# Luna attention and SiLU MLP on one core: other early order, w_out scaled without GpSimd, ones of v written once

## The chip, the core and the metric

The kernel runs on one core of a Trainium2 chip. Its engines are TensorE (PE, with its weight loads as PEld), VectorE (DVE), ScalarE (ACT), GpSimd (POOL) and SyncE (SP, which issues the DMAs). The metric is the device time of one execution in microseconds (us), the median of three runs; lower is better.

## The reference, cut to what matters

```
p_packed = softmax(p @ k.T / 8) @ v          # 8 batches x 8 heads, 576 tokens, head size 64, 32 packed rows
attn     = softmax(q @ p_packed.T / 8) @ p_packed
x        = attn, heads side by side           # 4608 tokens x 512
h        = x @ w_in                           # w_in 512 x 2048
g        = h * sigmoid(beta * h)              # beta: one number per hidden column
out      = g @ w_out                          # w_out 2048 x 512, float32
```

All inputs come as float32; the kernel multiplies in bfloat16 and adds up in float32.

## The kernel before, in words

The eight batches pass one after the other through the same steps, and neighbours overlap. In the names of the program, with b the batch:

- `ld` loads k, v and q of a batch, `cast` turns them to bfloat16 (k_bf, v_bf, q_bf). Batches 0 and 1 are cast by any of three engines and turned by PE (`tr`, `trr`, copied out by `T`, `rk`, `rq`); from batch 2 on POOL casts and a DMA transposes (`tr` on SP, tiles kT and qT).
- `s1`, `e1`, `pun`, `pp` form the packed rows; `s2`, `e2`, `z2`, `l2`, `n2`, `A2` the second softmax (tile A2T).
- `w`, `W`: the second attention product and the input product are fused: PE multiplies the packed rows with w_in (tile w_ps), DVE scales by beta into W_bf.
- `h`, `g`: for each of 16 blocks of 128 hidden columns PE computes A2T x W_bf (two matmuls of 512 columns, tile h_ps), ACT applies SiLU into g_main. `hr`, `gr` do the same for the 64 tokens left over.
- Output: batch 0 multiplies g by w_out plainly (`o`, with `take` and `add` on DVE). Batches 1 to 7 and the left-over tokens use a Strassen scheme with seven products (`p`, `P`): DVE first forms sums of blocks of w_out (`T4`, tile w_sum) and of g (`S`, tile g_sum), and reads the products out (`R`).

Since `W` holds beta, `w_out` is divided by it: each of 16 blocks of w_out is multiplied by `rbeta` while it is cast (line 1469, `cast_out`), on DVE, ACT or POOL. w_in and w_out come in four loads each (`ld_in`, `ld_out`) through three staging buffers, so a load waits until the casts of the load three places earlier are done.

What each engine does, and in which order, is written out by hand in the table `SEQUENCE`; a planner walks the five lists, and its estimated durations decide only how instructions of different engines are interleaved, where the activation tables are switched, and where PE gets fill products. `HOME` says from which ring of PSUM banks a step takes its bank: "h" (2 banks), "o" (2 banks) or "att" (4 banks). A fill product is a 128x128 matmul of ones whose result nobody reads; the planner puts some wherever it expects PE to wait in the first 60 us, if a bank of ring "o" is free:

```
if len(opened) >= n and (opened[-n][0] is None or opened[-n][0] > free["PE"]):
    return
...
        self.filler()
```

Each engine works its list strictly in order, SP too, and the wait of a list's head holds all that stands behind it. Lines 421 and 426 are helpers: every matmul has line 421 and every transpose on PE line 426.

Of the kernel before, what the change touches and what calls it, by code (L numbers as in the profile page):

```python
# [8 lines left out]
B, H, S, D = 8, 8, 576, 64  # L9
# [39 lines left out]
PE_BATCHES = 2  # L49
def TILED(key):  # L50
# [13 lines left out]
    ("brow", 0): "o",  # L64
    ("brow", 2): "o",
    ("brow", 3): "att",
    ("tr", 0, "q", 1): "h",
    ("s1r", 0): "o",
    ("s1", 0, 0): "h",
    ("s1", 0, 1): "h",  # L70
    ("z1", 0): "o",
    ("s2", 0, 1): "h",
    ("z2", 0, 0): "o",
    ("z2", 0, 1): "o",
    ("z2", 0, 2): "o",
    ("w", 0, 0): "o",
    ("tr", 1, "k", 0): "o",
    ("tr", 1, "k", 1): "h",
    ("tr", 1, "q", 0): "o",
    ("s1", 1, 1): "h",  # L80
    ("s2", 1, 0): "h",
    ("z2", 1, 0): "h",
    ("z2", 1, 1): "h",
# [305 lines left out]
class Kernel:  # L389
# [70 lines left out]
    def plan_loads(self, b):  # L460
        nc = self.nc
        rank = 100 * b
        early = b < PE_BATCHES
        for xi, x in enumerate("kqv" if b == 0 else "kvq"):
# [39 lines left out]
            old = self.readers(b - 1, x)  # L504
# [1047 lines left out]
```

## Time and profile before

| | |
|---|---|
| median of 3 runs | 240.79 us (240.64 to 241.34) |
| the profiled execution | 241.07 us |
| its span, first to last instruction | 239.3 us |
| around the span | 1.77 us |
| mean granted TensorE clock | 0.986 |
| last PE matmul ends | 235.6 us |

Durations in the text come from the profiled execution. Busy time is a sum over the span; what ends a wait is inferred from semaphores. A granted clock of 1.00 is the 2.4 GHz level of TensorE, 0.50 the 1.2 GHz level. "PE busy" is not PE at its peak: matmuls are pipelined, and one that is late counts as busy.

### The profile page before, as it was taken

The page shows a single profiled execution, that of the slowest core. Times are in us where ns is not written, and L with a number is a line of the kernel's source. Part 1 is how long each engine was busy: PE and PEld are TensorE (multiplying, and loading weights), DVE is VectorE, ACT ScalarE, POOL GpSimd, SP SyncE. Part 2 cuts the span into 40 slices and gives each one's busy share as a digit, 9 for nine tenths or more (in the row PEclk, how much of TensorE's full clock was granted, in tenths as well). Part 3 has the DMA queues.
Part 4 walks back from the last instruction along what each step waited for, and adds up shares of the span by engine and source line. Part 5 has one row for each costly group of instructions (what it writes and reads, how often), then busy time and mean ns, then how long its engine had stood idle before and what let it go on. Part 6 is the DMA issues. An engine that isn't in the chain of part 4 may idle for free.

```text
span 239.3 us, 6112 instructions
## 1 busy us (share of the span) xinstructions
PE 224.5 (94%) x2550; PEld 152.9 (64%) x2576; DVE 160.9 (67%) x254; ACT 171.3 (72%) x312; POOL 82.5 (34%) x90
## 2 busy tenths in 40 slices
PE   7887899986999999999999999999999999999993
PEld 6554353333477765775588567876786578677883
DVE  4569647884897945986798855852788279515751
ACT  3619679874899977977679678896788679665300
POOL 3223448398873160624151730540354000000000
PEclk9999589999999999999999999999999999999999
DMA  6999999999999999999999899969794040022044
GB/s 216 396 387 399 401 350 348 290 325 224 263 263 191 274 275 245 218 320 242 230 279 331 225 236 303 225 128 221 160 313 147 3 175 3 1 86 92 0 122 144
DMA packets 67107, 54.14 MB, mean 226 GB/s; under 512 B 38948, under 2 KB 58532, under 8 KB 66568
## 3 DMA queue, kind: packets, MB, share of 16 engines
q1 hardware_dynamic: 67072, 53.75, 81.5%
q8 instruction: 20, 0.33, 0.6%
q14 instruction: 7, 0.06, 0.1%
q10 hardware_dynamic: 8, 0.01, 0.0%
HBM read 37.23 MB, written 9.44 MB: 195 GB/s over the span
## 4 chain that ended last, share of the span: by engine, by line
PE 72%; DMA 11%; POOL 5%; ACT 4%; DVE 3%; issue 2%; SPq 1%; POOLq 0%; DVEq 0%
PE o_ps L421 42%; PE h_ps L421 19%; DMA k<-in_k_dram 6%; DMA w_in<-in_moe_w_in_dram 5%; POOL w_out_bf L1469 3%; PE w_ps L421 3%; PE hr_ps L421 3%; PE s_ps L421 2%; PE pp_ps L421 1%; PE z_ps L421 1%; ACT g_main L992 1%; POOL k_bf L515 1%; DVE g_main L1223 1%; DVE W_bf L957 1%; ACT L438 1%
## 5 line engine op out<-in xcount | busy, mean ns | idle before, releaser
L992 ACT ACTIVATE g_main<-h_ps 128x512 bf16<-128x512 f32 x128 | 72.2, 596 | 34.9 <-PE h_ps L421 28.1
L421 PEld LDWEIGHTS <-g_main 128*128 128x128 bf16 x624 | 58.8, 98 | 25.8 <-issue 5.3
L421 PE MATMUL h_ps<-A2T,W_bf 128*128 128x512 bf16 x233 | 68.5, 390 | 1.8 <-DVE A2T L890 1.0
L421 PE MATMUL o_ps<-w_out_bf,g_main 128*128 128x256 bf16 (+1 forms) x397 | 61.2, 289 | 2.3 <-POOL w_out_bf L1469 1.9
L421 PEld LDWEIGHTS <-W_bf 128*128 128x128 bf16 x512 | 33.2, 99 | 20.6 <-issue 6.6
L950 DVE TENSOR_TENSOR W_bf<-w_ps,beta_bc 128x512 bf16<-128x512 f32 x48 | 30.6, 684 | 15.8 <-PE w_ps L421 15.8
L421 PE MATMUL o_ps<-w_sum,g_sum 128*128 128x256 bf16 x256 | 33.1, 273 | 0.6 <-DVE o_sb L1253 0.4
L421 PE MATMUL o_ps<-w_sum,g_main 128*128 128x256 bf16 x224 | 31.3, 273 | 0.3
L1253 DVE TENSOR_TENSOR o_sb<-o_ps,o_sb 128x512 f32<-128x512 f32 (+1 forms) x27 | 17.0, 630 | 18.9 <-PE o_ps L421 15.6
L438 ACT ACT_TABLE_LOAD x22 | 28.2, 1283 | 1.1 <-PEq L1536 0.7
L421 PEld LDWEIGHTS <-g_sum 128*128 128x128 bf16 x256 | 24.3, 98 | 6.3 <-issue 1.0
L515 POOL CAST q_bf<-q 128x1024 bf16<-128x1024 f32 x12 | 13.6, 1151 | 31.2 <-DMA q<-in_q_dram 31.2
L515 POOL CAST v_bf<-v 128x1024 bf16<-128x1024 f32 x12 | 15.6, 1326 | 22.4 <-DMA v<-in_v_dram 22.4
L1255 ACT COPY o_sb<-o_ps 128x512 f32<-128x512 f32 (+1 forms) x16 | 8.1, 506 | 14.1 <-PE o_ps L421 14.1
L515 POOL CAST k_bf<-k 128x1024 bf16<-128x1024 f32 x12 | 13.3, 1124 | 12.8 <-DMA k<-in_k_dram 12.8
L1255 DVE COPY o_sb<-o_ps 128x512 f32<-128x512 f32 (+1 forms) x20 | 13.2, 661 | 4.1 <-PE o_ps L421 4.0
L957 DVE SCALAR_TENSOR_TENSOR W_bf<-w_ps,rz,beta_bc 128x512 bf16<-128x512 f32 x15 | 10.4, 745 | 4.2 <-PE w_ps L421 4.2
L890 DVE TENSOR_TENSOR A2T<-E2T,rz 128x512 bf16<-128x512 bf16 x16 | 11.6, 733 | 2.1 <-ACT rz L885 1.8
L1469 POOL TENSOR_SCALAR w_out_bf<-w_out,rbeta 128x512 bf16<-128x512 f32 x6 | 10.6, 1768 | 4.8 <-DMA w_out<-in_moe_w_out_dram 4.7
L1223 DVE TENSOR_TENSOR g_sum<-g_main 128x2048 bf16<-128x2048 bf16 x7 | 9.0, 1283 | 3.9 <-ACT g_main L992 3.9
L421 PE MATMUL w_ps<-w_in_bf,pp 64*32 64x512 bf16 x252 | 11.1, 389 | 0.0
L873 ACT ACTIVATE rz<-z_ps 128x512 f32<-128x512 f32 x16 | 9.6, 604 | 1.9 <-PE z_ps L421 1.9
(131 smaller groups left out, 281.3 us busy)
## 6 DMA issues: line engine op xcount, KB each, us to landing
k<-in_k_dram SPq DMA_DIRECT2D x6, 1024.0 KB, 8.7
v<-in_v_dram SPq DMA_DIRECT2D x6, 1024.0 KB, 8.3
q<-in_q_dram SPq DMA_DIRECT2D x6, 1024.0 KB, 9.2
out_dram<-o_sb SPq DMA_DIRECT2D x10, 512.0 KB, 3.7
w_in<-in_moe_w_in_dram SPq DMA_DIRECT2D x4, 1024.0 KB, 11.5
w_out<-in_moe_w_out_dram SPq DMA_DIRECT2D x4, 1024.0 KB, 10.7
out_dram<-o_sb SPq DMA_DIRECT2D x12, 256.0 KB, 3.8
k<-in_k_dram SPq DMA_DIRECT2D x4, 576.0 KB, 6.4
```

The costliest lines, as they stand in the source:

```text
L421: return self.nc.tensor.matmul(out, lhsT, rhs, start=start, stop=stop, tile_position=pos, skip_group_check=True)
L438: self.nc.scalar.preload_act_table_set(SETS[mode])
L515: self.copy[engine](o[:, 0 : 32 * e].rearrange("p (t h e) -> p h t e", t=4, h=8)[:, h, :, 0:D], t[:, 0:2048].rearrange("p (h t d) -> p h t ...
L873: nc.scalar.activation(st[b, "rz2"][:, i], ps[:], AF.Ln)
L890: nc.vector.tensor_tensor(part(st[b, "A2"], i), part(st[b, "E2"], i), st[b, "rz2"][:, i] if i < 2 else st[b, "rz2r"][:], ALU.mult)
L950: nc.vector.tensor_tensor(st[b, "W"][:, r, cols].rearrange("q (f p) -> q f p", f=4), st[b, "w", m][:].rearrange("q (p f) -> q f p", f=4), ...
L957: nc.vector.scalar_tensor_tensor(st[b, "W"][:, r, cols].rearrange("q (f p) -> q f p", f=4), st[b, "w", m][:].rearrange("q (p f) -> q f p", ...
L992: nc.scalar.activation(st[b, "g"][:, ft, :], st[b, "h", ft][:], AF.Silu)
L1223: nc.vector.tensor_tensor(o, x, y, op)
L1253: nc.vector.tensor_tensor(o, x, o, ALU.add)
L1255: self.copy[engine](o, x)
L1469: nc.scalar.mul(o, w, r) if engine == "ACT" else {"DVE": nc.vector, "POOL": nc.gpsimd}[engine].tensor_scalar_mul(o, w, r)
```

## The change: what it does

Five things are changed.

1. `HOME`: the early steps of batches 0 and 1 no longer take a bank of ring "o". They take "h" or "att", so that ring is left to the fill products until the first output product. The program has 176 fill products, before 84; 147 of them stand ahead of the first `h`, before 71.
2. `cast_out` and `put_out`: POOL no longer scales blocks of w_out. Before, DVE had 7 blocks, ACT 3 and POOL 6; now DVE has 12 and ACT 4. Some casts of k, q, v and w_in change their engine too: POOL now casts all of the first two loads of w_in and the first half of v of batch 1, DVE the first half of q and the second half of v of batch 1.
3. The column of ones that stands in v_bf behind each 64 columns of v (it sums the softmax) is written by POOL once, for batch 2, and not again for batches 3 to 7: the same tile is used on.
4. The lists of all five engines are new. In the first 70 us: k of batch 0 is loaded ahead of p; q of batch 2 is loaded and cast ahead of the rest of v; `h` of batch 1 starts between those of batch 0. Later places are shuffled by a few steps.
5. One estimate of the planner for DVE's w_out is 0.45 and not 0.4, one for the first cast of v of batch 2 is 1.35.

```diff
 HOME = {
-    ("brow", 0): "o",
-    ("brow", 2): "o",
...
-    ("w", 0, 0): "o",
+    ("w", 0, 0): "h",
+    ("w", 0, 2): "h",
...
-        ("ld", "p0"), ("ld", 0, "k", 0), ("ld", 0, "k", 1), ("ld", 0, "q", 0), ("ld", 0, "q", 1), ("ld", 0, "v", 0),
+        ("ld", 0, "k", 0), ("ld", 0, "k", 1), ("ld", "p0"), ("ld", 0, "q", 0), ("ld", 0, "q", 1), ("ld", 0, "v", 0),
...
-        ("ld", 2, "v", 0), ("ld", 2, "v", 2), ("ld", 2, "q", 0), ("ld", 2, "q", 2), ("tr", 2, "k", 0),
+        ("ld", 2, "v", 0), ("ld", 2, "q", 0), ("ld", 2, "q", 2), ("ld", 2, "v", 2), ("tr", 2, "k", 0),
...
                 t = self.t[b, x, "32"]
-                if i == 0:
+                if i == 0 and x == "v" and b > PE_BATCHES:
+                    self.t[b, x] = self.t[b - 1, x]
+                elif i == 0:
                     self.t[b, x] = self.inbf.tile([128, VW if x == "v" else 2304], bf16, tag=f"{x}bf", name=f"{x}_bf")
                     if x == "v":
                         nc.gpsimd.memset(self.t[b, x][:].rearrange("p (g e) -> p g e", e=VP)[:, :, D : D + 1], 1.0)
...
-            nc.scalar.mul(o, w, r) if engine == "ACT" else {"DVE": nc.vector, "POOL": nc.gpsimd}[engine].tensor_scalar_mul(o, w, r)
+            nc.vector.tensor_scalar_mul(o, w, r) if engine == "DVE" else nc.scalar.mul(o, w, r)
...
-                    self.task(("w_out", 4 * n + i), {"DVE": 0.4, "ACT": 0.7, "POOL": 0.8}, None, lambda e, i=i: cast_out(e, n, i), [ld, ("rbeta",)], rank)
+                    self.task(("w_out", 4 * n + i), {"DVE": 0.45, "ACT": 0.7}, None, lambda e, i=i: cast_out(e, n, i), [ld, ("rbeta",)], rank)
```

PE, just ahead of the first `h` of batch 0 (z2r_ps belongs to the second softmax, W_bf to the first block of `h`, w_ps is the second quarter of the fused weights). Before:

```order
L421 MATMUL s_ps<-pT,kT 64x64
L421 LDWEIGHTS bones [waits DVE_49]
L421 MATMUL z2r_ps<-E2T,bones 128x128 [waits Activation_49]
L421 LDWEIGHTS W_bf
L421 MATMUL h_ps<-A2T,W_bf 128x512
```

Now:

```order
L419 MATMUL s_ps<-pT,kT 64x64
L419 LDWEIGHTS ones
L419 MATMUL o_ps<-ones 128x128
...
L419 LDWEIGHTS bones [waits DVE_49]
L419 MATMUL z2r_ps<-E2T,bones 128x128 [waits Activation_49]
...
L419 MATMUL w_ps<-w_in_bf,pp 32x512 [waits Pool_49]
...
L419 LDWEIGHTS W_bf
L419 MATMUL h_ps<-A2T,W_bf 128x512 [waits DVE_49]
```

Eighteen fill products now stand between s_ps and z2r_ps, sixteen behind z2r_ps and four behind the eight matmuls of w_ps, which has moved ahead of the first `h` and waits for POOL's casts of w_in.

POOL, from the end of the casts of k of batch 2 to its first casts of q (the numbers in names are buffers: w_out_753 is the third load of w_out, w_out_822 the fourth). Before:

```order
L522 CAST k_bf<-k_702 128x256
L1418 CAST p_785<-p_785 96x1024
L1469 TENSOR_SCALAR w_out_bf<-w_out_753,rbeta 128x512
L1469 TENSOR_SCALAR w_out_bf<-w_out_822,rbeta 128x512 x2
L511 MEMSET v_bf 128x36
L515 CAST v_bf<-v_848 128x4x4x64
L515 CAST q_bf<-q_868 128x4x4x64 x2
```

Now:

```order
L522 CAST k_bf<-k_732 128x256
L1418 CAST p_865<-p_865 96x1024
L515 CAST q_bf<-q_932 128x4x4x64 x2
L522 CAST q_bf<-q_932 128x256
L511 MEMSET v_bf 128x36
L515 CAST v_bf<-v_926 128x4x4x64 x2
```

The three scalings are gone from here, and q stands ahead of v.

DVE, at the end of the fused weights of batch 1 (W_bf) and ahead of the sums of w_out blocks (w_sum). Before:

```order
L957 SCALAR_TENSOR_TENSOR W_bf<-w_ps,rz_618,beta_bc 128x512 x4
L1469 TENSOR_SCALAR w_out_bf<-w_out_753,rbeta 128x512
L1054 COPY o_sb<-o_ps 128x512
L1469 TENSOR_SCALAR w_out_bf<-w_out_753,rbeta 128x512
L1469 TENSOR_SCALAR w_out_bf<-w_out_822,rbeta 128x512
L1133 TENSOR_TENSOR w_sum<-w_out_bf 128x2048
```

Now:

```order
L1469 TENSOR_SCALAR w_out_bf<-w_out_836,rbeta 128x512 x2
L957 SCALAR_TENSOR_TENSOR W_bf<-w_ps,rz_724,beta_bc 128x512 x2
L1054 COPY o_sb<-o_ps 128x512
L1469 TENSOR_SCALAR w_out_bf<-w_out_836,rbeta 128x512 x2
L1469 TENSOR_SCALAR w_out_bf<-w_out_916,rbeta 128x512 x3
L1054 COPY o_sb<-o_ps 128x512
L1133 TENSOR_TENSOR w_sum<-w_out_bf 128x2048
```

DVE scales seven blocks of the last two loads here, before three.

## Rows read from the trace of the kernel before

**Rows 1.** The page's busy time of each engine, share of span, instructions.

```profile
PE 224.5 (94%) x2550; PEld 152.9 (64%) x2576; DVE 160.9 (67%) x254; ACT 171.3 (72%) x312; POOL 82.5 (34%) x90
```

**Rows 2.** Stretches: length, busy PE, PEld, DVE, ACT, POOL, then PEclk, DMA share, GB/s.

```profile
23.00:24.00 1.00, 0.04 (x1) 0.04 (x2) 1.00 (x3) 0.85 (x2) 1.00 (x1) 1.00 1.03 387
24.50:25.00 0.50, 0.00 (x0) 0.10 (x1) 0.50 (x2) 0.48 (x2) 0.00 (x0) 0.61 1.11 415
25.20:31.30 6.10, 6.09 (x38) 2.82 (x38) 3.88 (x8) 4.04 (x6) 2.42 (x3) 0.50 1.06 408
54.80:57.20 2.40, 0.50 (x4) 0.14 (x2) 0.27 (x1) 0.61 (x2) 2.40 (x4) 1.00 1.27 300
25.20:70.10 44.90, 41.54 (x383) 19.95 (x389) 32.73 (x51) 35.05 (x60) 32.24 (x28) 0.93 1.06 304
70.10:235.60 165.50, 163.84 (x1885) 119.28 (x1901) 111.92 (x162) 121.31 (x226) 41.86 (x48) 1.00 0.74 188
```

**Rows 3.** Instructions in time, first `h`: start, length, engine, [idle before and its releaser].

```profile
22.55 0.69 DVE L1458 CAST w_in_bf<-w_in 128x1024 bf16<-128x1024 f32 x1 [0.47 <-DMA w_in<-in_moe_w_in_dram]
22.58 1.56 POOL L1458 CAST w_in_bf<-w_in 128x1024 bf16<-128x1024 f32 x1 [1.64 <-DMA w_in<-in_moe_w_in_dram]
25.21 1.44 PE L421 MATMUL h_ps<-A2T,W_bf 128*128 128x512 bf16 x3 [1.02 <-DVE A2T L890]
26.58 0.63 PE L421 MATMUL w_ps<-w_in_bf,pp 64*32 64x512 bf16 x8
31.70 0.55 PE L421 MATMUL o_ps<-ones 128*128 128x128 bf16 x7
```

**Rows 4.** Instructions of ACT in time, SiLU of the first eight blocks and after.

```profile
28.45 0.60 ACT L992 ACTIVATE g_main<-h_ps 128x512 bf16<-128x512 f32 x1 [1.17 <-PE h_ps L421]
29.80 1.14 ACT L531 CAST v_bf<-v 128x1152 bf16<-128x1152 f32 x1
34.07 1.09 ACT L992 ACTIVATE g_main<-h_ps 128x512 bf16<-128x512 f32 x2 [0.97 <-PE qT_ps L426]
35.05 0.72 ACT L1469 ACTIVATE w_out_bf<-w_out,rbeta 128x512 bf16<-128x512 f32 x1
```

**Rows 5.** The tile w_out_bf: count, shortest/median/longest ns, first and last start.

```profile
L1469 DVE TENSOR_SCALAR w_out_bf<-w_out,rbeta x7: 471/656/925, 28.6 to 51.2; 128x512 bf16<-128x512 f32 x7
L1469 POOL TENSOR_SCALAR w_out_bf<-w_out,rbeta x6: 1557/1567/2625, 33.7 to 55.3; 128x512 bf16<-128x512 f32 x6
```

**Rows 6.** Instructions in time, last blocks of w_out and the first sum of g.

```profile
51.02 5.87 POOL L1469 TENSOR_SCALAR w_out_bf<-w_out,rbeta 128x512 bf16<-128x512 f32 x3
56.94 0.59 PE L421 MATMUL o_ps<-w_out_bf,g_main 128*128 128x512 bf16 x2 [1.90 <-POOL w_out_bf L1469]
66.30 1.59 DVE L1223 TENSOR_TENSOR g_sum<-g_main 128x2048 bf16<-128x2048 bf16 x1
```

**Rows 7.** Instructions in time, data of batches 2 and 3 on POOL, SP and PE.

```profile
59.01 3.02 POOL L515 CAST q_bf<-q 128x1024 bf16<-128x1024 f32 x2 [1.07 <-DMA q<-in_q_dram]
61.98 1.39 POOL L522 CAST q_bf<-q 128x256 bf16<-128x256 f32 x1
65.78 1.04 POOL L515 CAST k_bf<-k 128x1024 bf16<-128x1024 f32 x1 [1.07 <-DMA k<-in_k_dram]
63.39 3.36 SPq L597 DMA_TRANSPOSE qT<-q_bf  x1
70.16 3.17 SPq L597 DMA_TRANSPOSE kT<-k_bf  x1
71.54 0.41 PE L421 MATMUL s_ps<-qT,pp 64*32 64x512 bf16 x8
78.10 0.28 PE L421 MATMUL s1r_ps<-pT,kT 128*128 128x128 bf16 x2
```

**Rows 8.** DMA issues: count and median us from issue to landing.

```profile
kT<-k_bf SPq DMA_TRANSPOSE x6, 6.8
```

**Rows 9.** The chain that ended last, one Strassen product: start, length, what.

```profile
78.62 0.44 PE o_ps L421 x4
```

More of the change, by code (lines that the diff above doesn't have):

```diff
@@ L63 @@
 HOME = {
-    ("brow", 0): "o",
-    ("brow", 2): "o",
+    ("bcol",): "att",
+    ("brow", 0): "att",
+    ("brow", 1): "att",
     ("brow", 3): "att",
+    ("tr", 0, "k", 0): "h",
+    ("trr", 0, "k"): "h",
+    ("tr", 0, "q", 0): "h",
     ("tr", 0, "q", 1): "h",
[L68 to L75, printed above, removed]
-    ("w", 0, 0): "o",
[L77 to L81, printed above, removed]
+    ("s1r", 0): "h",
+    ("z2", 0, 1): "h",
+    ("z2", 0, 2): "h",
+    ("w", 0, 0): "h",
+    ("w", 0, 2): "h",
+    ("tr", 1, "k", 0): "h",
+    ("trr", 1, "q"): "h",
+    ("s1r", 1): "h",
     ("z2", 1, 0): "h",
-    ("z2", 1, 1): "h",
+    ("w", 1, 0): "h",
 }
@@ L87 @@
     "PE": [
[75 rows of a table removed]
[74 rows of a table added]
     ],
     "ACT": [
[37 rows of a table removed]
[37 rows of a table added]
     ],
     "DVE": [
[7 rows of a table removed]
-        ("W", 1, 6), ("W", 1, 7), ("w_out", 9), ("take", 0, 3), ("w_out", 11), ("w_out", 13), ("T4", 1),
[22 rows of a table removed]
[5 rows of a table added]
+        ("w_out", 7), ("W", 1, 0), ("w_in", 2, 1), ("take", 0, 0), ("W", 1, 1), ("take", 0, 2), ("W", 0, 4),
+        ("W", 0, 5), ("W", 1, 2), ("A2", 1, 0), ("W", 1, 3), ("A2", 1, 1), ("W", 1, 4), ("W", 1, 5), ("W", 0, 6),
+        ("W", 0, 7), ("w_out", 10), ("w_out", 8), ("W", 1, 6), ("W", 1, 7), ("take", 0, 1), ("w_out", 11),
+        ("w_out", 9), ("w_out", 13), ("w_out", 15), ("w_out", 12), ("take", 0, 3), ("T4", 1), ("pT1", 0, 0),
[22 rows of a table added]
     ],
     "POOL": [
-        ("cast", 0, "q", 0), ("cast", 0, "v", 0), ("cast", 1, "k", 0), ("w_in", 0, 0), ("w_in", 1, 1),
-        ("cast", 1, "q", 0), ("cast", 1, "q", 1), ("cast", 1, "v", 1), ("w_out", 4), ("pn", 1), ("w_out", 6),
-        ("w_in", 2, 1), ("w_in", 3, 1), ("w_in", 3, 0), ("cast", 2, "k", 0), ("w_out", 8), ("cast", 2, "k", 1),
-        ("cast", 2, "k", 2), ("p_bf",), ("w_out", 10), ("w_out", 15), ("w_out", 12), ("cast", 2, "v", 0),
[10 rows of a table removed]
+        ("p0_bf",), ("cast", 0, "q", 0), ("cast", 0, "v", 0), ("cast", 0, "v", 1), ("cast", 1, "k", 0),
+        ("cast", 1, "k", 1), ("pn", 0), ("w_in", 0, 1), ("w_in", 0, 0), ("w_in", 1, 1), ("w_in", 1, 0),
+        ("cast", 1, "q", 1), ("cast", 1, "v", 0), ("w_in", 2, 0), ("w_in", 3, 1), ("w_in", 3, 0), ("cast", 2, "k", 0),
+        ("cast", 2, "k", 1), ("cast", 2, "k", 2), ("p_bf",), ("cast", 2, "q", 0), ("cast", 2, "q", 1),
[10 rows of a table added]
     ],
     "SP": [
[1 row of a table removed]
[1 row of a table added]
         ("ld", 0, "v", 1), ("ld", 1, "k", 0), ("ld", 1, "k", 1), ("ld_in", 0), ("ld_in", 1), ("ld_out", 0),
@@ L255 @@
         ("ld_in", 3), ("ld", 2, "k", 0), ("ld", 2, "k", 2), ("ld_out", 2), ("ld", "p"), ("ld_out", 3),
[1 row of a table removed]
[1 row of a table added]
         ("ld", 3, "k", 0), ("ld", 3, "k", 2), ("tr", 2, "q", 0), ("ld", 3, "q", 0), ("tr", 3, "k", 0), ("store", 0),
[8 rows of a table removed]
-        ("store", 12), ("store", 11), ("store", 14), ("store", 13), ("store", 16, 0), ("store", "r1", 0),
-        ("store", "r1", 1), ("store", 17, 1), ("store", 16, 1), ("store", 17, 0),
[8 rows of a table added]
+        ("tr", 7, "q", 0), ("store", 11), ("store", 12), ("store", 14), ("store", 13), ("store", "r1", 0),
+        ("store", "r1", 1), ("store", 16, 0), ("store", 17, 1), ("store", 16, 1), ("store", 17, 0),
     ],
@@ L540, in plan_loads @@
             else:
-                c0 = self.task(("cast", b, x, 0), "POOL", 0.97, lambda f=piece: f("POOL", 0, 4), [m0] + old, rank + 3)
+                c0 = self.task(("cast", b, x, 0), "POOL", 1.35 if b == PE_BATCHES and x == "v" else 0.97, lambda f=piece: f("POOL", 0, 4), [m0] + old, rank + 3)
                 self.task(("cast", b, x, 1), "POOL", 0.97, lambda f=piece: f("POOL", 1, 4), [m0, c0], rank + 3)
```

315 rows, old and new, of the table SEQUENCE are left out of this document.

## The prediction, made before the changed kernel ran

> **What bounds the kernel now.** I read the busy times first: PE is busy 94% of the span, POOL 34% [rows 1]. Then the stretches [rows 2]. From 70.1 us, where the first Strassen product starts, to 235.6 PE is busy 163.84 of 165.50 us: only 1.66 us could be won there. From 25.2 (the first `h`) to 70.1 it is busy 41.54 of 44.90, which leaves 3.36 us idle, and in 25.2 to 31.3 it runs at a granted clock of 0.50, the 1.2 GHz level, for 6.10 us. Had the 6.09 us of work there run at 2.4 GHz, 3.05 would be saved at most. So the end of the kernel is set by when PE gets through this stretch, and by whether batches 2 and 3 then have their data; the slack in it is 3.36 + 3.05 = 6.4 us.
>
> What PE did before its clock fell stands in the same rows: 0.04 us of work in 23 to 24 and none in 24.5 to 25.0, where the clock goes from 1.00 to 0.61. It was waiting for the fused weights, which hang on w_in: the load lands at 22.55, the casts follow, and `h` starts at 25.21 [rows 3]. The second place is 54.8 to 57.2, where PE works 0.50 of 2.40 us and POOL all of it [rows 2]: POOL takes 5.87 us for its last three blocks of w_out, and PE waits 1.90 us for the last [rows 6].
>
> **The change part by part.** My sum is made against the profiled 241.07 us (239.30 of span, 1.77 around it), which is 0.28 above the median.
>
> *The start.* k ahead of p changes when the first casts run, but `h` hangs on w_in, behind the same bytes as before: 0. Just ahead of `h`, POOL now casts both halves of the second w_in load, and the fused weights made of it stand in front of `h`. From the landing at 22.55, two casts of at most 1.56 and 0.63 for the matmuls give 26.3 at the latest [rows 3]; at the earliest `h` starts at 25.2 as now, since its first weights and A2T are not later. I take 25.6, +0.4, as DVE no longer casts beside POOL there.
>
> *The fill products.* Between the last s_ps and `h` stand 38, where there were none. At 0.079 us each (0.55 for seven [rows 3]) they are 3.0 us, about the wait from 22.6 to 25.6. PE then works right up to `h`, and I expect the clock to stay at 1.00. Behind the first `h` stand 29 fills, before 13; the 16 more lie in waits for SiLU and cost nothing, or 16 x 0.079 = 1.3 us if those waits have gone.
>
> *SiLU of the first eight blocks.* ACT ends them at 35.16, after idle times for PE of 1.17, 0.97 and some shorter ones (2.1 or more in all), and a cast of v of 1.14 that now goes to POOL [rows 4]. Now: from 25.84 + 0.4, eight of 0.58 and two blocks of w_out of 0.72 make 6.1, so 32.3, 2.8 us earlier. Without the higher clock the idle 2.1 returns and 0.7 is left.
>
> *w_out off POOL.* DVE starts its block of the last load at 51.2, so that load has landed by then [rows 5]. DVE now has three of these blocks: 51.2 + 3 x 0.656 = 53.2, where POOL's last ends at 56.89 [rows 6]. The sums of w_out and the first sum of g, at 66.30, stand behind the same instructions, so they come 3.7 us earlier. DVE has five more scalings in all, 3.3 us; what hides them is its idle 44.90 - 32.73 = 12.2 us in the stretch [rows 2]. If that cover is gone, 0.4 is left; at the other end stands the whole slack of 6.4. I take 3.7, because the landing of the load, which the change cannot move much with DMA shares above 1.00 [rows 2], is the row nearest to it.
>
> *Data of batch 2.* What is late next is q. POOL starts its casts when it lands, at 59.01, and takes 4.36 us; the transposing DMA goes out at 63.39; PE's s_ps follows at 71.54, 8.15 us after [rows 7]. Such a transpose lands 6.8 us after its issue [rows 8], so 1.35 of the 8.15 are slack. An undisturbed cast takes 1.04 [rows 7], and these two take 3.02, beside DVE's sums of w_out. These come earlier now, and q stands ahead of v: the casts may save from 0 to 1.9 us; I take 1.4, as the sums will be nearly over. s_ps can then start at 62.0 + 6.8 = 68.8, 2.7 earlier, and by the new list PE has done two more products of 0.44 by then [rows 9]: 3.6 us of progress.
>
> The Trainium skill (SBUF — State Buffer, section Who interferes with whom) says that a DVE instruction with two SBUF inputs and a GpSimd instruction that reads SBUF exclude each other, and that the later one stops until the other has ended. The trace agrees, 3.02 us for two casts of 1.04. By that rule, if the sums still fell beside these casts, they would end at 63.4 as now, and the gain would be 1.35 + 0.9, about 2.2: 238.5 us.
>
> *The rest.* The ones of v saved on POOL and the new places after 70.1 I count as 0: POOL has 66% idle, PE 1.66 us. The new lists could win this 1.66; what they could lose no row shows, the nearest being the 3.36 idle of the early stretch.
>
> What reaches the end is the smallest of the gains in a row, 2.8 at SiLU (more of ACT's later waits go with w_out), 3.7 at w_out, 3.6 at batch 2: I take 3.6. 241.07 - 3.6 = 237.5, against the median 237.2 us.
>
> **The rivals.**
>
> 1. *The data chain of batches 2 and 3 takes it back.* The transpose of k of batch 3 goes out at 70.16 and PE needs it at 78.10 [rows 7]: with 6.8 us to land the slack is 1.1. For it: the DMA shares above 1.00. Against it: POOL gets to these casts sooner without w_out. If SP and POOL are no earlier, 240.79 - 1.1 = 239.7.
> 2. *The change does not do what it says: the clock falls all the same.* Fills stand where the planner expected waits, and a real wait may lie elsewhere. For it: the seven fills at 31.70 [rows 3] stood where the fall was already over, so the planner had misjudged the place once. Against it: 38 now stand in the very gap. 2.1 of the 3.6 go: 239.3.
> 3. *Slower: DVE becomes the bound.* If the five added scalings stand on its path to the last load, at the longest 0.925 [rows 5], it gets there at 51.2 + 4.6 and ends three blocks at 58.6, 1.7 after POOL's 56.89: 242.5. It decides against the change from the moment the last block is later than 56.89. For it: POOL's 10 us of scaling move to one engine that also keeps W_bf. Against it: 12.2 us idle.
> 4. *More than I take.* All of the early slack goes: 240.79 - 6.4 = 234.4. Against it: batch 2's landing at 59.
>
> **How the numbers follow.** The forecast gets 0.47, the data chain 0.17, the clock 0.10, DVE 0.14, more 0.12. A change below 0.3%, 0.7 us, can't be told from none here. Faster: 0.47 + 0.12 + 0.10 and 0.04 of the data chain, where it takes back only part, 0.73. Same: the other 0.13 of it, since 239.7 is close to the bound of 240.1 and the unknown lists can add half a microsecond. Slower: 0.14. The range goes from the full slack, 234.4, to 241.2, which is half a microsecond above no change: below it I leave 0.03, above it 0.12, most of the third rival. The forecast's own range is 235.8 to 238.6, the second bound from the casts that save nothing.
>
> **What would show it.** Clock: the stretch from the first `h` on at 1.00, and PE busy in the two microseconds ahead of it. SiLU: the eighth block ending near 32.3. w_out: the last scaling near 53, no wait of PE for it, the first sum of g near 62.6. Data: the first s_ps of batch 2 near 68.8, s1r_ps of batch 3 near 74.5, both with PE without long waits. From there to the last matmul, the same 164 to 166 us. The prediction is wrong if the first sum of g comes later than 66.3, if the clock falls again ahead of 60 us, or if PE reaches batch 3 early and then waits.

## The result: faster, 238.5 us where 237.2 was predicted

| | before | after |
|---|---|---|
| median, range | 240.79 us (240.64 to 241.34) | 238.49 us (237.21 to 240.78), 4 runs |
| ratio after to before | | 0.986, 95% interval 0.983 to 0.990 |
| the same, measured again beside the experiments | | 0.985 (0.980 to 0.990), median 237.97 us |
| profiled execution, its span | 241.07, 239.3 us | 238.53, 236.7 us |
| last PE matmul ends | 235.6 us | 233.0 us |

The ratios are against executions of the kernel before that ran beside each kernel, and they leave out an execution more than 1.5% above the fastest of its kernel, here the one of 240.78, while medians and ranges have them all. The medians alone give 0.990 for the first row and 0.983 for the repetition (237.97 against 242.02), so the size of the gain is known to half a per cent only. The forecast of 237.2 is a ratio of 0.985 to 240.79. The time is inside the range of 234.4 to 241.2 and 1.3 us above the forecast; the profiled execution gained 2.5 us where the sum had 3.6.

### The profile page after: what moved, and what is told of

The parts are those of the page before. It is cut to its first block, busy times and chain, and to the rows that moved or that the text cites. A ratio compares the mean times of both kernels' runs of the same rounds, so it can differ in the third digit from the quotient of the medians.

```text
span 236.7 us, 6282 instructions
## 1 busy us (share of the span) xinstructions
PE 226.3 (96%) x2642; PEld 157.4 (67%) x2668; DVE 158.5 (67%) x255; ACT 169.6 (72%) x312; POOL 70.9 (30%) x84
## 4 chain that ended last, share of the span: by engine, by line
PE 75%; DMA 14%; SPq 2%; DVE 2%; POOL 2%; ACT 1%; issue 1%; POOLq 0%; ACTq 0%
PE o_ps L419 44%; PE h_ps L419 19%; DMA w_in<-in_moe_w_in_dram 5%; DMA w_out<-in_moe_w_out_dram 5%; PE hr_ps L419 3%; DMA v<-in_v_dram 3%; PE w_ps L419 3%; PE s_ps L419 2%; DMA k<-in_k_dram 2%; PE pp_ps L419 1%; PE z_ps L419 1%; POOL w_in_bf L1458 1%; SPq L483 1%; DVE g_main L1223 1%; SPq L490 1%
## 5 line engine op out<-in xcount | busy, mean ns | idle before, releaser
L992 ACT ACTIVATE g_main<-h_ps 128x512 bf16<-128x512 f32 x128 | 71.1, 595 | 32.4 <-PE h_ps L419 23.6
L419 PE MATMUL h_ps<-A2T,W_bf 128*128 128x512 bf16 x235 | 65.5, 379 | 0.7 <-issue 0.2
L419 PE MATMUL o_ps<-w_out_bf,g_main 128*128 128x256 bf16 (+1 forms) x395 | 59.9, 289 | 1.0 <-DVE o_sb L1255 0.5
L419 PEld LDWEIGHTS <-W_bf 128*128 128x128 bf16 x512 | 32.6, 98 | 19.5 <-issue 3.7
L419 PE MATMUL o_ps<-w_sum,g_sum 128*128 128x256 bf16 x256 | 34.3, 273 | 0.1
L419 PE MATMUL o_ps<-w_sum,g_main 128*128 128x256 bf16 x224 | 30.4, 273 | 0.2
L419 PE MATMUL o_ps<-ones 128*128 128x128 bf16 x176 | 14.5, 238 | 1.1 <-DVE ones L1302 1.1
L419 PEld LDWEIGHTS <-ones 128*128 128x128 bf16 x176 | 12.2, 108 | 3.1 <-issue 1.2
L957 DVE SCALAR_TENSOR_TENSOR W_bf<-w_ps,rz,beta_bc 128x512 bf16<-128x512 f32 x16 | 11.3, 742 | 1.8 <-PE w_ps L419 1.6
```

The source lines that it names most:

```text
L419: return self.nc.tensor.matmul(out, lhsT, rhs, start=start, stop=stop, tile_position=pos, skip_group_check=True)
L957: nc.vector.scalar_tensor_tensor(st[b, "W"][:, r, cols].rearrange("q (f p) -> q f p", f=4), st[b, "w", m][:].rearrange("q (p f) -> q f p", ...
L992: nc.scalar.activation(st[b, "g"][:, ft, :], st[b, "h", ft][:], AF.Silu)
```

## The profile after

The page's busy time (engine, us, share of the span, instructions), which answers to [rows 1]:

```profile
PE 226.3 (96%) x2642; PEld 157.4 (67%) x2668; DVE 158.5 (67%) x255; ACT 169.6 (72%) x312; POOL 70.9 (30%) x84
```

The stretches, with the columns of [rows 2]:

```profile
23.00:24.00 1.00, 1.00 (x25) 0.96 (x20) 1.00 (x2) 0.88 (x3) 1.00 (x2) 1.00 1.04 402
25.20:31.30 6.10, 5.99 (x69) 3.99 (x72) 5.55 (x10) 5.41 (x9) 2.43 (x2) 1.00 1.04 399
48.00:50.00 2.00, 0.00 (x0) 0.00 (x0) 2.00 (x5) 0.49 (x2) 1.04 (x1) 1.00 0.93 335
54.80:57.20 2.40, 2.40 (x13) 1.09 (x12) 1.93 (x4) 2.08 (x5) 0.00 (x0) 1.00 1.79 210
25.20:70.10 44.90, 42.17 (x439) 22.04 (x446) 37.21 (x63) 36.47 (x62) 19.01 (x19) 1.00 1.09 311
70.10:233.00 162.90, 160.93 (x1862) 117.17 (x1865) 106.66 (x160) 119.09 (x222) 37.68 (x42) 1.00 0.78 189
```

Both holes of the kernel before are closed: 25.2 to 31.3 runs at the 2.4 GHz level, and 54.8 to 57.2 is full. But a new one is there: from 48 to 50 PE does nothing at all. The instructions in time show what it waits for (start, length, engine, and in brackets the idle time before and its releaser), first on POOL, then on PE:

```profile
48.94 1.04 POOL L1418 CAST p<-p 96x1024 bf16<-96x1024 f32 x1 [3.92 <-DVE W_bf L957]
50.04 0.51 PE L424 MATMUL pT_ps<-identr,p 96*128 96x96 bf16 x8 [2.19 <-POOL p L1418]
```

POOL idles 3.92 us ahead of this cast. The releaser named, W_bf, isn't an input of it; its input is the load of p, and in the other profiled execution of the same list the row names that load. The load goes out at 37.82 and lands 11.0 us later, at 48.8 (from tile and queue, KB, us from issue to landing):

```profile
37.82 0.36 SPq L1414 DMA_DIRECT2D p<-in_p_dram  x1
p<-in_p_dram SPq DMA_DIRECT2D x1, 384.0 KB, 11.0
```

In the kernel before it stood otherwise. The load went out at 39.20 and landed 9.2 us later, at 48.4, but POOL was busy without a gap from 46.97, with a scaling of w_out and two casts of k, and cast p only at 49.81:

```profile
39.20 0.35 SPq L1414 DMA_DIRECT2D p<-in_p_dram  x1
p<-in_p_dram SPq DMA_DIRECT2D x1, 384.0 KB, 9.2
46.97 1.56 POOL L1469 TENSOR_SCALAR w_out_bf<-w_out,rbeta 128x512 bf16<-128x512 f32 x1 [3.31 <-DMA w_out<-in_moe_w_out_dram]
48.48 1.04 POOL L515 CAST k_bf<-k 128x1024 bf16<-128x1024 f32 x1
49.81 1.23 POOL L1418 CAST p<-p 96x1024 bf16<-96x1024 f32 x1
51.09 0.51 PE L426 MATMUL pT_ps<-identr,p 96*128 96x96 bf16 x8 [0.71 <-POOL p L1418]
```

PE now comes to the transposes of p at 47.85 and not at 50.38, 2.5 us earlier; the cast comes only 0.87 earlier, because now the landing holds it and no longer POOL. The rest became a wait. The other steps, in the order of [rows 3 to 7]:

```profile
25.69 0.81 PE L419 MATMUL h_ps<-A2T,W_bf 128*128 128x512 bf16 x3
31.41 1.09 ACT L992 ACTIVATE g_main<-h_ps 128x512 bf16<-128x512 f32 x2 [0.45 <-PE h_ps L419]
51.25 1.28 DVE L1469 TENSOR_SCALAR w_out_bf<-w_out,rbeta 128x512 bf16<-128x512 f32 x3 [0.39 <-DMA w_out<-in_moe_w_out_dram]
58.00 2.57 POOL L515 CAST q_bf<-q 128x1024 bf16<-128x1024 f32 x2 [8.02 <-DMA q<-in_q_dram]
60.53 0.39 POOL L522 CAST q_bf<-q 128x256 bf16<-128x256 f32 x1
60.95 4.56 SPq L597 DMA_TRANSPOSE qT<-q_bf  x1
64.01 1.29 DVE L1223 TENSOR_TENSOR g_sum<-g_main 128x2048 bf16<-128x2048 bf16 x1
69.83 0.41 PE L419 MATMUL s_ps<-qT,pp 64*32 64x512 bf16 x8
76.60 0.28 PE L419 MATMUL s1r_ps<-pT,kT 128*128 128x128 bf16 x2
```

The eighth SiLU ends at 32.50 (before 35.16), the last scaling at 52.53 (before 56.89), the transposes of q go out at 60.95 (before 63.39). All of that came within 0.2 us of the prediction or ahead of it. But the first sum of g is only 2.29 us earlier, s_ps of batch 2 1.71 with two more products done, and s1r_ps of batch 3 1.50.

## The experiments

Theory A: what was gained ahead of 48 us is used up by the wait for p, so the scaling of w_out is the part that reaches the end. The rivals: the clock at the first `h` is; the order of batch 2's data is. Ratios are to the kernel before, measured beside each. The lists in the edits are cut to the places that moved.

| kernel | median us | ratio, 95% interval |
|---|---|---|
| before + new HOME | 241.48 | 1.000 (0.997 to 1.003) |
| before + new HOME, fewer fills | 240.69 | 0.998 (0.995 to 1.001) |
| before + w_out off POOL | 238.54 | 0.989 (0.986 to 0.992) |
| changed, again | 237.97 | 0.985 (0.980 to 0.990) |
| changed, no fills in the gap | 238.81 | 0.990 (0.986 to 0.994) |
| changed, w_out of the last load on POOL | 240.22 | 0.993 (0.990 to 0.996) |
| changed, p later | 237.14 | 0.983 (0.978 to 0.987) |
| the same, again | 237.04 | 0.983 (0.980 to 0.985) |
| p later, no fills in the gap | 237.43 | 0.982 (0.978 to 0.986) |
| p later, v ahead of q | 238.16 | 0.985 (0.981 to 0.989) |
| p later, w_out of the last load on POOL | 240.84 | 0.993 (0.989 to 0.996) |
| p later, ones of v for each batch | 237.26 | 0.984 (0.981 to 0.987) |

### The changed kernel without the fills ahead of the first `h`

```diff
     def keep_warm(self):
...
+        self.fills = getattr(self, "fills", 0) + 1
+        if 109 < self.fills <= 147:
+            return
         self.mm(self.warm[:, 0:128], self.ones[:], self.ones[:])
```

> The changed kernel without the 38 fill products between the last s_ps and the first h of batch 0; all else as changed. Theory A (the clock's gain is used up at the wait for p): in 24.5 to 25.0 the granted clock falls below 0.8 and the stretch behind the first h runs at 0.50 for about 6 us; the eighth SiLU ends 2 to 3 us later than the 32.50 of the changed kernel, near 35; PE then reaches the transposes of p near 50 instead of 47.85, at about the time when the cast of p has ended anyway, so its wait of 2.19 us shrinks to under 0.7; the end comes at 238.5 to 239.2. Rival B (the clock's gain reaches the end): 241 us, ratio to the kernel before 1.00. Rival C (the fills do not hold the clock): the clock stays at 1.00, the eighth SiLU ends near 32.5, and the time is 238.5 within 0.5.

The time is near theory A's, the reason isn't. The stretches of this kernel, columns as before:

```profile
23.00:24.00 1.00, 0.23 (x1) 0.18 (x2) 1.00 (x3) 1.00 (x4) 1.00 (x2) 1.00 1.06 408
25.20:31.30 6.10, 6.10 (x62) 3.41 (x61) 5.33 (x10) 5.18 (x10) 2.42 (x2) 1.00 1.05 400
48.00:50.00 2.00, 0.13 (x3) 0.14 (x4) 2.00 (x4) 0.32 (x1) 1.04 (x1) 0.98 0.95 361
50.00:53.00 3.00, 3.00 (x20) 1.88 (x19) 1.93 (x5) 1.43 (x3) 0.00 (x0) 0.50 1.07 345
```

The clock stayed at 1.00 at the first `h` without a fill in the gap: the new order has the second w_ps in it, and the waits left there are 0.50 and 0.84 us where the kernel before waited 1.18 and 1.02. So rival C is right there. The first `h` comes at 24.88, 0.81 earlier than with the fills, which thus overran the wait they were to fill. But PE waits 2.20 us for p all the same, and this time its clock falls behind that wait, to 0.50 from 50 to 53, where in the changed kernel's profiled execution it stayed at 1.00 behind one of 2.19. Four of the six executions have a mean clock of 0.990 to 0.993; they took 238.56 to 239.83 us, the other two 238.77 and 238.86, so here the fall shows no price.

### The kernel before with the new HOME alone

Edit: the table HOME of the changed kernel, nothing else.

> The kernel before with the new table HOME alone: fill products stand in the gap ahead of the first h, the lists and the scaling of w_out by GpSimd stay as before. Theory A: the clock stays at 1.00 from the first h on and the eighth SiLU ends 2 to 3 us earlier than 35.16, but PE still waits for the last scaling of w_out near 56.9 (its wait grows from 1.90 to 3 or more), so the time is 240.3 to 241, ratio 0.998 to 1.000. Rival B (the clock alone made the gain): 238.5, ratio 0.99. Rival C: the clock falls as before and nothing changes at all, 240.8 with the eighth SiLU near 35.

The ratio is theory A's, but not cleanly: 209 fills now, whose number the planner takes from its own estimates, pushed the first `h` to 28.41, and the eighth SiLU ended at 35.84. The clock was kept and its gain spent. The last experiment below repairs this.

### The last scalings of w_out back on POOL

The line of `cast_out` takes POOL again, and the lists change:

```diff
 "DVE":
-        ("w_out", 13), ("w_out", 15), ("w_out", 12), ("take", 0, 3), ("T4", 1), ...
+        ("take", 0, 3), ("T4", 1), ...
 "POOL":
-        ("p_bf",), ("cast", 2, "q", 0), ...
+        ("p_bf",), ("w_out", 13), ("w_out", 15), ("w_out", 12), ("cast", 2, "q", 0), ...
```

> The changed kernel with the three scalings of the last load of w_out (blocks 12, 13, 15) back on GpSimd, ahead of the casts of q of batch 2. Theory A (w_out decides): the last scaling ends at 56.9 to 57.5 instead of 52.53, PE waits for it 1.5 to 4 us, the first sum of g starts near 66 instead of 64.01, and the time is 240 to 241, ratio 0.997 to 1.003. Rival B (the order of the data of batches 2 and 3 decides, q ahead of v): q lands near 58.0 in either case, so the transposes of q still go out near 61 and the time stays at 238.5 to 239, ratio 0.986 to 0.992.

The time of 240.22 us is theory A's, but the ratio of 0.993 lies between the two, nearer to rival B's bound of 0.992. POOL ends at 55.66, the first sum of g starts at 66.32, PE did not wait for w_out: it came late itself, since its clock fell behind the wait for p (0.50 in 52 to 53). Two causes are mixed, so the same edit is repeated below without the wait for p.

### p later

```diff
 "PE":
-        ("p_tr",), ("h", 0, 14), ("h", 1, 9), ("o", 0, 2, 9), ("o", 0, 3, 7),
-        ("h", 1, 10), ("o", 0, 2, 11), ("h", 1, 4), ("o", 0, 1, 9), ("h", 1, 2), ("h", 1, 5), ("o", 0, 2, 13),
+        ("h", 0, 14), ("h", 1, 9), ("o", 0, 3, 7), ("h", 1, 10), ("h", 1, 4),
+        ("o", 0, 2, 9), ("h", 1, 2), ("o", 0, 2, 11), ("h", 1, 5), ("p_tr",), ("o", 0, 1, 9), ("o", 0, 2, 13),
 "DVE":
-        ("w_out", 8), ("W", 1, 6), ("W", 1, 7), ("take", 0, 1), ("w_out", 11), ("w_out", 9),
+        ("w_out", 8), ("w_out", 9), ("w_out", 11), ("W", 1, 6), ("W", 1, 7), ("take", 0, 1),
 "ACT":
-        ("w_out", 14), ("g", 1, 9), ("g", 1, 10), ("g", 1, 4), ("g", 1, 2), ("g", 1, 5),
+        ("g", 1, 9), ("g", 1, 10), ("g", 1, 4), ("g", 1, 2), ("g", 1, 5), ("w_out", 14),
```

> The changed kernel with the transposes of p nine products later in TensorE's list, with blocks 9 and 11 of w_out scaled ahead of two blocks of W_bf on VectorE, and block 14 five SiLUs later on ScalarE, so that nothing in front waits for p. Theory A: the wait of 2.19 us for p goes, PE stands 1.5 to 2.7 us further at 55 us; the transposes of k of batch 3 (out at 68.55, needed 6.8 later) leave only 1.25 of it, so the time is 237.0 to 237.6, ratio 0.983 to 0.987 of the kernel before. Rival B (PE has all its data in time): the whole 2.2 to 2.7 reach the end, 236, ratio 0.978. Rival C (q of batch 2 decides, landing at 58.0 whatever PE does): 238.5, ratio 0.990, with a new wait of PE near 67 for q's transposes.

Theory A, at 237.14 us. Its stretches, and the steps in time:

```profile
48.00:50.00 2.00, 1.78 (x9) 0.69 (x8) 2.00 (x4) 1.60 (x4) 1.04 (x1) 1.00 1.01 379
50.00:53.00 3.00, 3.00 (x15) 1.35 (x14) 2.48 (x6) 2.52 (x5) 0.00 (x0) 1.00 1.07 344
25.20:70.10 44.90, 44.01 (x454) 22.97 (x452) 39.40 (x65) 38.25 (x67) 18.92 (x19) 1.00 1.09 314
```

```profile
53.22 0.51 PE L424 MATMUL pT_ps<-identr,p 96*128 96x96 bf16 x8
62.63 1.48 DVE L1223 TENSOR_TENSOR g_sum<-g_main 128x2048 bf16<-128x2048 bf16 x1
68.38 0.41 PE L419 MATMUL s_ps<-qT,pp 64*32 64x512 bf16 x8
67.70 4.28 SPq L597 DMA_TRANSPOSE kT<-k_bf  x1
75.15 0.27 PE L419 MATMUL s1r_ps<-pT,kT 128*128 128x128 bf16 x2
```

The wait is gone, and the first sum of g (62.63), s_ps (68.38) and s1r_ps (75.15) stand within 0.7 us of the prediction's 62.6, 68.8 and 74.5: its sum would have held had p not been in the way. The transposes of k of batch 3 leave 75.15 - 67.70 - 6.8 = 0.65 us of slack by [rows 8], 1.35 by this trace's own median of 6.1, and PE is busy 44.01 of 44.90 us, so little is left here. The same kernel was run once more:

> The kernel with p later once more. Theory A (it is faster than the changed kernel because neither the wait for p nor the clock's fall behind it is left): 0.980 to 0.985 of the kernel before, mean clock 0.998 or more in all executions, times spread over 2 us at most. Rival B (its first result was chance): 0.985 or above.

Theory A: 237.04 us. These are the two lowest medians of all. Against the changed kernel the intervals overlap; a difference of 0.3% is likely and not settled.

### The changed kernel again

> The changed kernel once more, beside the three variants of the kernel with p later, to compare on one chip. Theory A (the wait for p makes TensorE's clock fall in part of its executions): ratio to the kernel before 0.984 to 0.992, its times spread over 2 us or more as in its first four (237.21 to 240.78), and if the profiled execution shows a mean clock below 0.998, the fall stands between 48 and 53 us. Rival B (its times are the same from execution to execution, and the spread came from the chip): a spread under 1 us and a ratio within 0.002 of 0.986.

Theory A in ratio (0.985) and spread (3.2 us); the cause that it names is not shown. Of its six executions four with a mean clock of 1.00 took 236.85 to 238.04, two with 0.993 took 239.43 and 240.05. But among the first four of this kernel the one of 240.78 has a mean clock of 1.00, so a long time also comes without a fall. With p later all twelve executions have a clock of 0.997 or more and lie between 236.43 and 238.50. That the fall in those two stood behind the wait for p is not shown by their own traces; it is where the traces of two variants have it (columns as before, the one without fills in the gap and the one with w_out on POOL):

```profile
51.00:52.00 1.00, 1.00 (x4) 0.34 (x3) 0.89 (x3) 0.43 (x1) 0.00 (x0) 0.50 1.08 346
```

```profile
52.00:53.00 1.00, 1.00 (x12) 1.00 (x10) 0.00 (x0) 0.39 (x1) 1.00 (x2) 0.50 1.09 348
```

### p later, without the fills in the gap

Edit: the one on the fills above, in the kernel with p later.

> The kernel with p later (237.14 us, ratio 0.983) without the 38 fill products ahead of the first h. Theory A (the new order alone holds the clock there, and the fills delay the first h): clock 1.00 from 24.5 on, first h near 24.9 to 25.2 where it was 25.5 to 26.1 with them, and no wait of PE above 1 us between 44 and 60; the 0.6 us reach PE at 47 but p and the last load of w_out land no earlier, so the end is 236.5 to 237.2, ratio 0.979 to 0.984. Rival B (without fills the clock falls in some executions): mean clock near 0.986 in the profile and a ratio of 0.985 to 0.990. Rival C: no difference at all, 0.983 within 0.002.

The clock holds (1.00 in 25.2 to 31.3), the first `h` comes at 24.66, and the end does not move: ratio 0.982. So by its median the 38 fills are worth nothing in this order and cost nothing. But one of its six executions took 241.98 us at a mean clock of 0.991, while the 24 with p later and these fills (the two above, v ahead of q, and ones of v for each batch) all have 0.996 or more and 238.74 at most; one in six is too few to say whether the fills prevent that. PE is earlier and then waits 0.62 us for the transposed k of batch 2 and 0.49 for an output bank.

### p later, v ahead of q

```diff
 "SP":
-        ("ld", 2, "v", 0), ("ld", 2, "q", 0), ("ld", 2, "q", 2), ("ld", 2, "v", 2),
+        ("ld", 2, "v", 0), ("ld", 2, "v", 2), ("ld", 2, "q", 0), ("ld", 2, "q", 2),
 "POOL":
-        ("cast", 2, "q", 0), ("cast", 2, "q", 1), ("cast", 2, "q", 2), ("cast", 2, "v", 0),
+        ("cast", 2, "v", 0), ("cast", 2, "q", 0), ("cast", 2, "q", 1), ("cast", 2, "q", 2),
```

> The kernel with p later, with the old order of batch 2: the whole of v loaded ahead of q, and the first half of v cast ahead of q on GpSimd. Theory A (q's place is worth part of the gain): the casts of q start about 1.0 later than 57.64, the transposes of q go out at 62.0 to 63.4 instead of 61.03 and land 6.8 later, 68.8 to 70.2, so s_ps of batch 2 cannot start at 68.38; PE waits 0.4 to 1.8 us for them and the time is 237.6 to 239, ratio 0.985 to 0.991. Rival B (there is slack in q): no wait, the ratio stays at 0.983 within 0.002.

The casts of q start at 58.81 and the transposes go out at 62.21, 1.2 us later; with 6.8 to land [rows 8] that is 69.0, and s_ps starts at 68.96, 0.58 later than with p later, behind a wait of 0.77. The row puts that wait down to a result of DVE, which ends at the same time, but with p later s_ps starts without waiting for it. At 0.985 against 0.983 q's place is worth about 0.6 us by the trace, less than the intervals can tell.

### p later, the last scalings on POOL

Edit: the one on the scalings above, in the kernel with p later.

> The kernel with p later, with the three scalings of the last load of w_out back on GpSimd: the same undoing as before on the changed kernel, now without the wait for p in front of it. Theory A (w_out is worth as much without that wait and its clock): the last scaling ends near 55.6 instead of 52.1, the first sum of w_out starts at 56 instead of 52.62, the first sum of g at 65 to 66 instead of 62.63, and the time is 1.5 to 2.5 above that with p later, 238.6 to 239.6, ratio 0.989 to 0.994. Rival B (what the undoing cost before was the clock's fall at 51 to 53): within 0.7 us of the kernel with p later, ratio under 0.986.

Theory A in the ratio: 0.993 against 0.983, some 2.4 us. The rows on PE and DVE:

```profile
56.86 0.59 PE L419 MATMUL o_ps<-w_out_bf,g_main 128*128 128x512 bf16 x2 [3.35 <-POOL w_out_bf L1469]
56.84 1.23 DVE L1133 TENSOR_TENSOR w_sum<-w_out_bf,w_sum 128x2048 bf16<-128x2048 bf16 x1 [3.16 <-POOL w_out_bf L1469]
```

The old wait is back, and longer, because PE comes to it sooner. How much of the 2.4 us is the wait alone is not settled: nine of the twelve executions have a mean clock of 0.993 or less, and the median of 240.84 is above theory A's 239.6. The profiled execution, with a clock of 1.00, took 239.59, 3.0 more than the profiled one with p later (236.62).

### The kernel before with w_out off POOL alone

```diff
 "POOL":
-        ("w_out", 4), ("pn", 1), ("w_out", 6), ... ("w_out", 8), ... ("w_out", 10), ("w_out", 15), ("w_out", 12),
+        ("pn", 1), ...
 "DVE":
-        ("w_out", 5), ... ("W", 1, 6), ("W", 1, 7), ("w_out", 9), ("take", 0, 3), ("w_out", 11), ("w_out", 13),
+        ("w_out", 5), ("w_out", 4), ("w_out", 6), ... ("w_out", 8), ("W", 1, 6), ("W", 1, 7), ("w_out", 9),
+        ("w_out", 10), ("take", 0, 3), ("w_out", 11), ("w_out", 13), ("w_out", 15), ("w_out", 12),
```

> The kernel before with one part of the change alone: the six scalings of w_out that GpSimd did (blocks 4, 6, 8, 10, 15, 12) stand in VectorE's list; all else in its old order. Theory A (this part is the main one): TensorE no longer waits 1.90 us for the last scaling, which ends near 53 to 54.5 instead of 56.89; GpSimd gets to v and q of batch 2 sooner; the first sum of g starts near 64 to 65 instead of 66.30 and the time is 238.8 to 239.8, ratio 0.989 to 0.994. Rival B (the old order of batches 2 and 3 holds the end back): the wait goes but comes back before 80 us for q's or k's transposes, and the time is 240.5 to 241.5, ratio 0.997 to 1.000. Rival C (VectorE becomes the bound, the slower side of the forecast): the last scaling ends after 56.9 and the ratio is above 1.003.

Theory A, and a little more: 238.54 us, 0.989. This one part, in the old order and with the old HOME, makes 1.1% of the change's 1.4 to 1.5; the intervals overlap, so whether the other parts add anything is open. PE no longer waits for w_out at all, and p is cast when it lands and not 1.1 us later. Its stretch at the first `h`, the cast of p, and the scaling:

```profile
25.20:31.30 6.10, 6.10 (x52) 3.24 (x51) 4.46 (x8) 4.17 (x7) 2.56 (x2) 0.72 1.05 401
```

```profile
48.71 1.04 POOL L1418 CAST p<-p 96x1024 bf16<-96x1024 f32 x1 [2.95 <-DMA p<-in_p_dram]
51.13 1.66 DVE L1469 TENSOR_SCALAR w_out_bf<-w_out,rbeta 128x512 bf16<-128x512 f32 x4
```

The clock did fall behind the first `h` (0.72), and it cost nothing that the end shows.

### p later, ones of v for each batch

Edit: the memset of the kernel before, for each of batches 2 to 7.

> The kernel with p later, with the ones of v written again by GpSimd for each of batches 3 to 7, as the kernel before did. Theory A (this part is worth nothing, since GpSimd is idle two thirds of the span): ratio to the kernel before 0.981 to 0.985, the same as with p later (0.983), GpSimd 5 more instructions of 0.25 us. Rival B (GpSimd's casts of batches 3 to 7 stand on the path, and a write of ones makes the casts of v wait for the last reader of the batch before): 0.5 us or more later, ratio 0.985 or above.

0.984 and a span of 234.6 us, against 234.7 and 235.0 with p later: no difference.

### The new HOME with fewer fills

```diff
+        self.fills = n = getattr(self, "fills", 0) + 1
+        if 59 < n <= 143 or 151 < n <= 158 or 166 < n <= 175 or 187 < n <= 203:
+            return
```

> The kernel before with the new HOME alone, as run before, but with 116 of its 209 fill products ahead of the first h left out: those kept are about as many as the kernel before had, and 20 more (8 and 12, 1.6 us in all) in the gap right ahead of the first h, so that they no longer push it to 28.41. Theory A (the clock's fall at the first h costs nothing at the end, since PE waits later for w_out in any case): first h at 25 to 25.7, the granted clock 1.00 in 25.2 to 31.3, the eighth SiLU ends at 32 to 33.5 instead of 35.16, PE's wait for the last scaling of w_out grows from 1.90 to 3 us or more, and the ratio to the kernel before is 0.996 to 1.002. Rival B (the clock's gain reaches the end): 1 us or more faster, ratio 0.988 to 0.993. Rival C (these fills are too few): the clock falls as before, 1.00.

Theory A. The rows on PE, ACT and the stretch:

```profile
24.11 1.10 PE L419 MATMUL h_ps<-A2T,W_bf 128*128 128x512 bf16 x3
31.70 1.08 ACT L993 ACTIVATE g_main<-h_ps 128x512 bf16<-128x512 f32 x2
51.84 0.51 PE L424 MATMUL pT_ps<-identr,p 96*128 96x96 bf16 x8 [1.50 <-POOL p L1419]
57.05 0.59 PE L419 MATMUL o_ps<-w_out_bf,g_main 128*128 128x512 bf16 x2 [1.25 <-POOL w_out_bf L1470]
66.33 1.21 DVE L1224 TENSOR_TENSOR g_sum<-g_main 128x2048 bf16<-128x2048 bf16 x1
```

```profile
25.20:31.30 6.10, 5.06 (x68) 3.00 (x69) 4.96 (x9) 4.42 (x9) 2.30 (x2) 1.00 1.05 401
```

The clock is held, the eighth SiLU ends at 32.78, 2.4 us earlier, and the first sum of g stands at 66.33 where it was 66.30. The gain went into longer waits for p (1.50, behind POOL's scalings, which move p's cast to 50.75) and for w_out (three, 2.5 in all, though the last of them is shorter than before and not longer, as theory A had it). Ratio 0.998, its interval just reaching 1: 0.5% at most.

## Why the prediction was right, and where it was not

**Right in sign, and in what carries it.** The sum took w_out off POOL for 3.7 us, the largest of its terms, and that part alone gives 1.1%, 2.7 us. It acts at two places: the wait of 1.90 us for the last scaling goes, and p's cast, which stood behind a scaling on POOL, comes 0.87 us earlier. The sum had the first place only; the two were not tested apart.

**The step that failed** is "What is late next is q". What was late next was p. The prediction followed `h`, w_out, q and k, and put nothing for p. It left out that the new list has the transposes of p ahead of products that need nothing of them, at a place that PE now reaches 2.5 us sooner, while p doesn't land sooner: at 48.8, where it was 48.4. Its cast starts at 48.94, and between 48.47 and 48.90 in the nine other traces of the changed kernel and its variants. The wait of 0.71 us in the trace of before was a wait for POOL, and the landing, 1.4 us ahead of that cast, was the next bound. Now PE waited 2.19 us there, and of the 3.6 us of the sum 2.5 reached the end. With p later the later steps come where the prediction had them.

**First `h`**: 25.6 predicted, 25.69, which was luck: the sum had it from POOL's casts, but without the 38 fills it comes at 24.88, so the fills set it. **Clock**: 1.00 as predicted, but by the order as much as by the fills; in the profiled executions fills alone do it in the old order, and the order does it without fills. **SiLU**: 32.3 predicted, 32.50. That this and w_out and batch 2 stand in a row, and the smallest gain reaches the end, was a wrong model for the clock's share. By these words the smallest was 2.8, and the sum took 3.6. And in the kernel before none of it gets past POOL, which waits for a load of w_out until 46.97 and then works without a gap to 56.89; in the two kernels with the new HOME alone this starts at 47.46 and 47.72, though PE is earlier in one of them. In the 67 executions of the kernel before that the ratios of these experiments use, the mean clock is below 0.988 in 25, from 0.988 to 0.995 in 24 and above in 18; the medians of these are 242.0, 241.4 and 242.0 us. Where in each of them the clock fell is not on record.

**w_out**: the last scaling at 53.2 predicted, 52.53. The term was right, but DVE's price was mis-sized. One scaling takes 481 ns and not the 656 of [rows 5]:

```profile
L1469 DVE TENSOR_SCALAR w_out_bf<-w_out,rbeta x12: 476/481/487, 24.9 to 52.1; 128x512 bf16<-128x512 f32 x12
```

The longer ones of before (to 925 ns) stood beside a cast or a scaling on POOL, which came first. Of the twelve only the one at 27.82 has a POOL instruction beside it, a cast that started later, at 28.02, and took 1.28 where its like takes 1.15. So DVE's twelve take 12 x 0.481 = 5.8 us where its seven took about 7 x 0.656 = 4.6, 1.2 more and not 3.3; the third rival had its price from rows that POOL had lengthened. The Trainium skill (SBUF — State Buffer, section Who interferes with whom) says that a DVE tensor_scalar can run in a mode which takes the port pair shared with GpSimd, and that the one that issues later then stops until the other is done. The trace agrees, with 656 ns or more behind a cast or a scaling of POOL and 476 ahead of one.

**q**: the casts were to save 1.4 us of 4.36; they took 60.92 - 58.00 = 2.92, so 1.44. q itself landed 1.0 earlier, which was not in the sum. With 6.2 us to land (the median of this trace) the transposed q is there at 67.2, 2.7 us ahead of s_ps, so q was not late any more. The rule of the same section of the Trainium skill, weighed in the prediction as 238.5 us, was seen at work with p later: the cast of 0.39 took 1.39 beside a sum of w_out (59.18 to 60.74).

```profile
59.61 1.39 POOL L522 CAST q_bf<-q 128x256 bf16<-128x256 f32 x1
59.18 1.56 DVE L1133 TENSOR_TENSOR w_sum<-w_out_bf,w_sum 128x2048 bf16<-128x2048 bf16 x1
```

In the changed kernel the casts took 2.92 us where that case has 4.36, so the case did not come about. That the time of 238.49 fell near its 238.5 is luck: what held the end back was the wait for p.

**The rest**: the stretch from 70.1 took 162.90 us with 160.93 busy, as little idle as before (1.97 and 1.66); it is shorter by the work that PE had done sooner. The ones of v: 0 predicted, 0 found. **The rivals**: none of the four happened as written. The second had a mechanism that is seen at another place: in the traces of two variants the clock falls behind the wait for p. Where it fell in the two of ten executions of the changed kernel that have a lower clock (0.993) is not on record.

## What to carry to other kernels

Follow every wait that PE makes after the one that is removed, the small ones too, and look what stands behind it: a wait of 0.7 us for a busy engine hid a load that had landed only 1.4 us before, and with the engine free and PE 2.5 us earlier it became a wait of 2.2 for the load. A clock that falls ahead of a step that PE doesn't move was free here. Whether a fall behind it is paid is not settled: 2 us lie between two executions with it and four without in one kernel, nothing in another. Take the price of a moved instruction from rows where its old partner isn't running beside it.

## What was not expected of the hardware

- Behind a wait of about 2.2 us at the same place the granted clock stayed at 1.00 in one execution and fell to 0.50 for some 3 us in another, of two kernels that differ in the 38 fills. The length of the wait alone doesn't decide it: behind 2.02 us the clock fell (last scalings back on POOL), and behind 3.35 us it stayed at 1.00 (the same with p later).
- p landed at nearly the same time in the two kernels (48.4 and 48.8 us) though its load went out 1.4 us earlier in the second.
- 38 fill products can delay the product behind them: the first `h` came at 25.69 with them and at 24.88 without, with POOL's casts of w_in ending at the same time (24.46 and 24.48).
